# New durations, hand-over times and a new transfer rate in the table of an attention-and-feed-forward kernel's scheduler

## The chip, the core and the metric

The kernel runs on one core of one Trainium2 chip. It uses TensorE (PE in the profile; its weight loads are PEld), VectorE (DVE), ScalarE (ACT), GpSimd (POOL) and SyncE (SP), which here issues nearly all transfers. The metric is the device time of one execution in microseconds, as the median of several runs.

## What is computed

Two layers, one behind the other. The first is linear attention with random features, on 8 batch entries of 8 heads, 576 positions and 64 dimensions:

```python
def phi(x):
    proj = np.einsum('bhsd,md->bhsm', x, omega)
    sq = np.sum(x * x, axis=-1, keepdims=True) / 2.0
    h = proj - sq
    h = h - np.max(h, axis=-1, keepdims=True)
    return np.exp(h) / np.sqrt(m)
q_p, k_p = (phi(q_s), phi(k_s))
kv = np.einsum('bhsm,bhsd->bhmd', k_p, v)
z = np.sum(k_p, axis=2)
num = np.einsum('bhsm,bhmd->bhsd', q_p, kv)
den = np.einsum('bhsm,bhm->bhs', q_p, z)[..., None] + 1e-06
return (num / den).astype(np.float32)
```

The second takes the attention's output as 4608 tokens of 512 values and puts them through a feed-forward layer with 2048 inner values:

```python
h = x @ w_in
sp = np.maximum(h, 0.0) + np.log1p(np.exp(-np.abs(h)))
g = h * erf(sp)
return (g @ w_out).astype(np.float32)
```

## The kernel before

**Tiling.** The heads are taken in pairs, four pairs to each of the 8 batch entries, 32 pairs in all. For a pair, `load` brings keys and queries (uk, uq) and values (v) and squares them into the other half of the same tile (`sqk`, `sqq`). `project` multiplies in three groups of 384 rows (PSUM tiles ppk, ppq), takes the row maxima (mxk, mxq on DVE) and the exponentials (fk, fq on ACT). `key_values` sums keys times values (kvp, copied to kh, kl). `turn` transposes the query features (pt, copied to qh, with the remainder ql). `attend` multiplies both (nd), takes the reciprocal (rc, on ACT as logarithm and exponential) and divides (xs, on DVE).

The feed-forward layer runs for each batch entry in two phases of four blocks. Operands are split in a high part and a remainder (xh and xl, gh and gl, and both in each weight tile w), and each product is three matmuls: high by high, high by low, low by high. The first three batch entries multiply in the plain way (`plain1`, tiles h). From the fourth on, `gemm1` uses a Strassen scheme with seven products (tiles hS and hA, helper u). `chain` then computes softplus and erf (gs, on ACT, with table loads), the gate (hs), and the split. `gemm2` multiplies by the output weights (tiles o, copied or added to os, stored by `ostore`). The weights are unpacked once in `make` (a load to st, a bias to wt, three steps in pw, then `parts` into w), stored to DRAM, and fetched again from there for every later use (`fetch`).

**What sets the order.** No order is written out by hand. `build` lists every operation with the engines that may run it, a duration for each (the second number of each option) and a slack from which that option may be used. `Plan.order` then plays the program through: it keeps a time for each engine, gives each idle engine the ready operation that is due first, and writes down the sequence. An operation becomes ready after its producers, plus LAG of the producing engine. PSUM banks and buffers are handed out in the same play: a new tile waits until all users of a freed one are done. For SP it assumes that a transfer ends 2 us after a bandwidth clock (`bw`) that advances by size over a rate. The program is then emitted in that sequence, each engine in order, with `keep_in_program_order`. So durations in the table don't set any time on the chip; they set which engine runs an operation, which operation stands ahead of which on an engine, and which PSUM bank and buffer a tile gets.

**Lines of the profile.** All instructions are recorded by one helper, so nearly every row has line L755; rows are told apart by the names of their tiles. Buffer numbers are left out in the profile.

Of the kernel before, what the change touches and what calls it, by code (L numbers as in the profile page):

```python
# [59 lines left out]
LAG = {"T": 0.35, "A": 0.25, "V": 0.25, "G": 0.3, "S": 0.3}  # L60
# [29 lines left out]
class Plan:  # L90
# [43 lines left out]
    def order(self, slots, caps):  # L134
# [192 lines left out]
def build(emit):  # L327
# [36 lines left out]
    def parts(t, src, keys, psum=False):  # L364

        ks = range(2)
        pl.op("whigh", [("A", 0.58, -1e9), ("V", 0.62, WHV)] if psum else
              [("A", 0.63, -1e9), ("G", 0.7, WHG)], lambda e: E.w_high(e, t, src),
              reads=keys, writes=[(t, ("h", k)) for k in ks])
        pl.op("wlow" if psum else "wrest",  # L370
              [("V", 0.68, -1e9)] if psum else [("V", 0.68, -1e9), ("G", 1.3, 3.0)], lambda e: E.w_rest(e, t, src),
              reads=keys + [(t, ("h", k)) for k in ks], writes=[(t, ("l", k)) for k in ks])

    def make(u, t):
# [6 lines left out]
        pl.op("wbias", [("G", 0.8, WBG), ("A", 0.67, -1e9)], lambda e: E.w_bias(e, st, w),  # L381
# [5 lines left out]
        pl.op("wsign", [("V", 0.72, -1e9)], lambda e: E.w_sign(st, p), reads=[(st, 0), (p, 0)],  # L387
# [19 lines left out]
    def make_sums(ph, fp, t0, t1):  # L407

        r = pl.tile("gh", f"R{ph}_{fp}", [P, 2, 2, BW], F32, "wt")
        for i, t in enumerate((t0, t1)):  # L410
            pl.op("wwhole", [("V", 0.68, -1e9), ("G", 1.3, 3.0)],
                  lambda e, i=i, t=t: E.w_whole(e, r.ap[:, i], t),
                  reads=[(t, (x, k)) for x in "hl" for k in range(2)], writes=[(r, i)])
        s = pl.tile("gl", f"S{ph}_{fp}", [P, 4, BW], F32, "st")

        for x, y, sign, keys, to in (
# [4 lines left out]
            pl.op("wsum", [("V", 0.37, -1e9), ("G", 0.75, 3.0)],  # L421
# [51 lines left out]
    def project(n, qk, t0):  # L473
# [5 lines left out]
        for i in range(3):  # L479
# [4 lines left out]
            pl.op("max" + qk, [("V", 0.56, -1e9)], lambda e, i=i, pp=pp: E.maximum(mx, pp, i),  # L484
                  reads=[(pp, 0)], writes=[(mx, i)])
            pl.op("exp" + qk, [("A", 1.1, -1e9)], lambda e, i=i, pp=pp: E.exponential(f, mx, pp, i),
                  reads=[(pp, 0), (mx, i)], writes=[(f, i)], set="exp")

    def key_values(n, t0):
# [10 lines left out]
        pl.op("kvhigh", [("V", 0.6, -1e9), ("A", 0.7, -1e9)], lambda e: E.kv_high(e, kh, kvp),  # L500
              reads=[(kvp, 0)], writes=[(kh, 0)])
        if not whole:
            pl.op("kvrest", [("V", 0.6, -1e9)], lambda e: E.kv_rest(kl, kvp, kh),
                  reads=[(kvp, 0), (kh, 0)], writes=[(kl, 0)])

    def turn(n, t0):
# [5 lines left out]
        for i in range(3):  # L512
# [3 lines left out]
            pl.op("turnhigh", [("A", 0.5, -1e9), ("V", 0.5, -1e9)],  # L516
                  lambda e, i=i, pt=pt: E.turn_high(e, qh, pt, i), reads=[(pt, 0)], writes=[(qh, i)])
            if not whole:
                pl.op("turnrest", [("V", 0.56, -1e9)], lambda e, i=i, pt=pt: E.turn_rest(ql, qh, pt, i),
                      reads=[(pt, 0), (qh, i)], writes=[(ql, i)])  # L520

    def attend(n, t0):
        a = pairs[n]
        x = xs[n] = pl.tile("xs", f"xs{a['nm']}", [P, 2, T])
        for t in range(2):
# [83 lines left out]
    def plain1(b, ph, fp):  # L609
# [3 lines left out]
        for i in range(2):  # L613
            for t in range(2):
# [3 lines left out]
                pl.op("hout", [("A", 0.42, -1e9), ("V", 0.46, 0.0)],  # L618
# [3 lines left out]
    def gemm1(b, ph, fp):  # L622
# [25 lines left out]
    def chain(b, ph, fps):  # L648
# [25 lines left out]
    def gemm2(b, ph, et):  # L674
# [378 lines left out]
```

## Time and profile before

| | |
|---|---|
| time, median of 3 runs | 1087.89 us (1086.58 to 1088.42) |
| span of the profiled execution, first to last instruction | 1083.2 us |
| its own time beside the span | not listed; the median is 4.7 us over the span |
| transfers | 231.27 MB, 213 GB/s on average |
| fetches of 512 KB weight tiles, issue to landing | 4.4 us in the median (184 of them) |
| table loads on ACT | 91, 1283 ns each |

The profile is of one execution. A row of the timeline gives start, length, engine, line, operation, output and inputs, the count of instructions merged, and in brackets the idle time of the engine ahead of it with what ended it. Matmul ends are modelled, so the start of the next matmul tells more than the end of the last. In the windows a row gives the stretch, its length, the busy time of PE, PEld, DVE, ACT and POOL with instruction counts, the granted TensorE clock, the DMA engines' share and the GB/s moved.

### The profile page before, as it was taken

Reading aid. Unit: us, or ns where it says so; the run is one execution under the profiler, and the core shown is the slowest. Engines: PE = TensorE matmul, PEld = TensorE weight load, DVE = VectorE, ACT = ScalarE, POOL = GpSimd, SP = SyncE. Lnnn points to the kernel's source line nnn. Section 1 sums busy time; section 2 is a strip of 40 time slices with the busy share of each in tenths; the row PEclk is TensorE's granted clock in tenths of the full one; section 3 lists DMA queues with packets and bytes.
Section 4 is the critical chain, followed back from the end, with each engine's and each line's share of the span. In section 5 each row is a group of like instructions: output and inputs, shape, how many; then the busy total and the mean of one; then the engine's idle time right before and its main releaser. Section 6 shows DMA issues by size and latency. Waiting matters only on the chain.

```text
span 1083.2 us, 21493 instructions
## 1 busy us (share of the span) xinstructions
PE 1066.8 (98%) x8272; PEld 1059.2 (98%) x8272; DVE 724.0 (67%) x1302; ACT 672.6 (62%) x1262; POOL 462.6 (43%) x362
## 2 busy tenths in 40 slices
PE   7899999999999999999999999999999999999998
PEld 7799999999999999999999999999999999999998
DVE  5999988683585676946667565766657757565541
ACT  7768876576676685647647555675556665564440
POOL 5436336352294673815335334452435412253300
PEclk9999999999999999999999999999999999999999
DMA  8465676676367676568765766667765766667771
GB/s 235 162 210 177 221 265 223 227 274 200 115 218 240 225 234 202 177 206 255 226 208 183 248 226 223 187 211 233 230 210 182 241 203 197 216 229 265 264 240 52
DMA packets 70117, 231.27 MB, mean 213 GB/s; under 512 B 8288, under 2 KB 8672, under 8 KB 70016
## 3 DMA queue, kind: packets, MB, share of 16 engines
q1 hardware_dynamic: 69952, 229.84, 64.9%
q8 instruction: 66, 1.08, 0.4%
q14 instruction: 35, 0.29, 0.1%
q0 software_dynamic: 64, 0.07, 0.0%
HBM read 195.26 MB, written 34.60 MB: 212 GB/s over the span
## 4 chain that ended last, share of the span: by engine, by line
PE 94%; DVE 4%; ACT 1%; issue 0%; DMA 0%; DVEq 0%; POOLq 0%
PE o L755 37%; PE h L755 14%; PE hS L755 12%; PE hA L755 9%; PE ppk L755 6%; PE ppq L755 6%; PE kvp L755 5%; PE nd L755 5%; PE pt L755 2%; DVE mxk L755 0%; DVE xl L755 0%; DVE pw L755 0%; DVE gl L755 0%; DVE xc L755 0%; DVE qh L755 0%
## 5 line engine op out<-in xcount | busy, mean ns | idle before, releaser
L755 PE MATMUL o<-gh,w 128*128 128x288 f32 x2048 | 442.3, 298 | 1.9 <-DVE ql L755 1.0
L755 PEld LDWEIGHTS o<-gh,w 128*128 128x128 f32 x2048 | 338.3, 188 | 2.5 <-PE o L755 1.2
L755 PE MATMUL o<-gl,w 128*128 128x288 f32 x1024 | 301.8, 295 | 0.0
L755 PEld LDWEIGHTS o<-gl,w 128*128 128x128 f32 x1024 | 192.7, 188 | 0.1
L755 PE MATMUL h<-xh,w 128*128 128x288 f32 x768 | 176.0, 303 | 0.6 <-DVE hs L755 0.6
L755 PE MATMUL hS<-xh,wS 128*128 128x288 f32 x640 | 160.0, 299 | 1.1 <-DVE u L755 1.1
L755 POOL TENSOR_TENSOR hs<-gs,hs 128x576 f32<-128x576 f32 x64 | 101.4, 1607 | 105.7 <-ACT gs L755 68.9
L755 POOL TENSOR_TENSOR gl<-hs,gh 128x576 fp32r<-128x576 f32 x66 | 117.9, 1810 | 33.0 <-ACT gh L755 25.7
L755 PEld LDWEIGHTS h<-xh,w 128*128 128x128 f32 x768 | 129.1, 188 | 1.5 <-DVE hs L755 0.8
L755 ACT ACTIVATE fk<-ppk,mxk 128x128 f32<-128x128 f32 x288 | 82.2, 375 | 74.8 <-DVE mxk L755 74.5
L755 PE MATMUL hA<-xh,w 128*128 128x288 f32 x480 | 122.8, 300 | 0.0
L755 ACT ACT_TABLE_LOAD x91 | 116.8, 1283 | 4.3 <-DVE hs L755 2.0
L755 PEld LDWEIGHTS hS<-xh,wS 128*128 128x128 f32 x640 | 112.9, 188 | 1.3 <-DVE u L755 1.3
L755 POOL TENSOR_TENSOR uq<-uq 64x576 f32<-64x576 f32 x42 | 49.7, 1201 | 150.3 <-DMA uq<-qT 105.3
L755 PE MATMUL h<-xl,w 128*128 128x288 f32 x384 | 113.0, 294 | 0.0
L755 ACT ACTIVATE fq<-ppq,mxq 128x128 f32<-128x128 f32 x288 | 81.6, 372 | 30.4 <-DVE mxq L755 30.2
L755 DVE TENSOR_REDUCE mxk<-ppk 128x3 f32<-128x384 f32 x96 | 52.4, 555 | 62.6 <-PE ppk L755 61.3
L755 PE MATMUL hS<-xl,wS 128*128 128x288 f32 x320 | 94.2, 294 | 0.0
L755 POOL TENSOR_TENSOR uk<-uk 64x576 f32<-64x576 f32 x46 | 52.4, 1159 | 86.1 <-DMA uk<-kT 60.8
L755 PEld LDWEIGHTS hA<-xh,w 128*128 128x128 f32 x480 | 85.5, 188 | 0.1
L755 DVE TENSOR_TENSOR os<-o,os 128x288 f32<-128x288 f32 x64 | 29.0, 455 | 83.5 <-PE o L755 83.5
L755 PE MATMUL ppk<-wk,uk 128*128 128x128 f32 x576 | 78.1, 280 | 4.1 <-DVE wk L755 4.0
(94 smaller groups left out, 2084.6 us busy)
## 6 DMA issues: line engine op xcount, KB each, us to landing
w<-wdw SPq DMA_DIRECT2D x184, 512.0 KB, 4.4
wS<-wdcS SPq DMA_DIRECT2D x80, 512.0 KB, 4.0
st<-w SPq DMA_DIRECT2D x32, 512.0 KB, 4.5
wdw<-w SPq DMA_DIRECT2D x32, 512.0 KB, 4.2
v<-vP SPq DMA_DIRECT2D x32, 325.0 KB, 3.6
w<-wdw SPq DMA_DIRECT2D x40, 256.0 KB, 3.5
out<-os SPq DMA_DIRECT2D x32, 288.0 KB, 3.5
uk<-kT SPq DMA_DIRECT2D x31, 288.0 KB, 3.8
```

Source lines behind the costliest of these rows:

```text
L755: return tc.keep_in_program_order(method(*args, **kwargs))
```

## The change

The table gets new numbers, and nothing else is touched. LAG of ACT, DVE and POOL goes up, the rate of transfers goes from 230 to 300 KB per us, most durations of DVE and ACT go down by 0.05 to 0.3 us, and some of POOL go up. The core of the diff:

```diff
-LAG = {"T": 0.35, "A": 0.25, "V": 0.25, "G": 0.3, "S": 0.3}
+LAG = {"T": 0.35, "A": 0.35, "V": 0.33, "G": 0.33, "S": 0.3}
...
-                        bw = begin + o.size / 230e3
+                        bw = begin + o.size / 300e3
...
-            pl.op("max" + qk, [("V", 0.56, -1e9)], lambda e, i=i, pp=pp: E.maximum(mx, pp, i),
+            pl.op("max" + qk, [("V", 0.47, -1e9)], lambda e, i=i, pp=pp: E.maximum(mx, pp, i),
```

In the same way: exponentials 1.1 to 0.77, `turnhigh` on ACT 0.5 to 0.39, `kvhigh` 0.6 and 0.7 to 0.4, evacuations of PSUM on DVE 0.46 to 0.38 and on ACT 0.42 to 0.34, `sp` and `erf` 1.2 to 1.1, `wbias` on POOL 0.8 to 0.65, `rest` on POOL 2.75 to 2.95, `recip` 1.45 to 1.5.

This moves operations between engines (`turnhigh` on ACT from 37 to 58 of 96, `wbias` on ACT from 5 to 17 of 32) and shifts rows on all of them. Three places follow. In their names the first number of a pair's tile is the pair within its batch entry (qh_0 is pair 0; weights wt, st and w have other numbers), the last a running number.

ACT, in the first batch entry, from the square of a later key tile to the exponentials of pair 1's queries. Before:

```order
L755 ACTIVATE uk_0_118<-uk_0_118 64x1152
L755 ACTIVATE fk_1_214<-ppk_1_0_187,mxk_1_200 128x128 x3
L755 ACTIVATE qh_0_229<-pt_0_1_218 128x384
L755 ACTIVATE fk_1_214<-ppk_1_1_196,mxk_1_200 128x128 x3
L755 ACTIVATE fk_1_214<-ppk_1_2_203,mxk_1_200 128x128 x3
L755 ACTIVATE uq_0_141<-uq_0_141 64x1152
L755 ACTIVATE rc_0_0_266<-nd_0_0_0_233,eps 64x288
L755 ACTIVATE rc_0_0_266<-nd_0_1_0_238,eps 64x288
L755 ACTIVATE rc_0_0_266<-rc_0_0_266 128x288
L755 ACTIVATE fq_1_276<-ppq_1_0_249,mxq_1_258 128x128 x3
```

With the change, from the row behind the same square on:

```order
L755 ACTIVATE uk_2_126<-uk_2_126 64x1152
L755 ACTIVATE fk_1_222<-ppk_1_0_187,mxk_1_201 128x128 x3
L755 ACTIVATE qh_0_230<-pt_0_2_226 128x384
L755 ACTIVATE fk_1_222<-ppk_1_1_197,mxk_1_201 128x128 x3
L755 ACTIVATE fk_1_222<-ppk_1_2_203,mxk_1_201 128x128 x3
L755 ACTIVATE wt_0_0_250<-st_0_0_150 128x512
L755 ACTIVATE rc_0_0_256<-nd_0_0_0_234,eps 64x288
L755 ACTIVATE rc_0_0_256<-nd_0_1_0_239,eps 64x288
L755 ACTIVATE rc_0_0_256<-rc_0_0_256 128x288
L755 ACTIVATE rc_0_1_275<-nd_0_0_1_246,eps 64x288
L755 ACTIVATE rc_0_1_275<-nd_0_1_1_248,eps 64x288
L755 ACTIVATE rc_0_1_275<-rc_0_1_275 128x288
```

The three exponentials fq_1 come directly behind these, then the square of uq_3 and the bias wt of the third weight tile, then fk_2. A second square and a weight bias came to ACT (from POOL), and both reciprocals now stand ahead of fq_1.

DVE, from the third weight tile's first step to the copies of pair 2's turned queries. Before:

```order
L755 TENSOR_SCALAR pw_0_2_454<-wt_0_2_375 128x512
L755 TENSOR_REDUCE mxk_3_460<-ppk_3_0_437 128x3
L755 TENSOR_REDUCE mxk_3_460<-ppk_3_1_448 128x3
L755 COPY qh_2_479<-pt_2_0_462 128x384
L755 COPY qh_2_479<-pt_2_1_467 128x384
L755 TENSOR_REDUCE mxk_3_460<-ppk_3_2_456 128x3
L755 SCALAR_TENSOR_TENSOR pw_0_2_454<-st_0_2_297,pw_0_2_454 128x512 x2
```

With the change:

```order
L755 TENSOR_SCALAR pw_0_2_440<-wt_0_2_343 128x512
L755 SCALAR_TENSOR_TENSOR pw_0_2_440<-st_0_2_297,pw_0_2_440 128x512 x2
L755 TENSOR_REDUCE mxk_3_461<-ppk_3_0_442 128x3
L755 TENSOR_REDUCE mxk_3_461<-ppk_3_1_452 128x3
L755 TENSOR_REDUCE mxk_3_461<-ppk_3_2_457 128x3
L755 COPY qh_2_485<-pt_2_0_463 128x384
L755 COPY qh_2_485<-pt_2_2_480 128x384
```

All three weight steps and all three maxima now stand ahead of the copies. A little later on ACT, the square of a query tile of the second batch entry (uq_1) comes to stand directly ahead of the two reciprocals of pair 3, where before no square stood.

PE, at the step from the plain to the Strassen batches, from the last turn of a pair to its products nd. Before, 13 rows of the output tile o lie between; these are the last five with the product behind them:

```order
L755 MATMUL o_0_3_1_5503<-gl_0_2_4716,w_0_3_1_88_5193 128x288
L755 MATMUL o_0_3_1_5503<-gh_0_2_4638,w_0_3_1_88_5193 128x288
L755 MATMUL o_0_3_1_5503<-gh_0_3_4746,w_0_3_1_88_5193 128x288
L755 MATMUL o_0_3_1_5503<-gl_0_3_4791,w_0_3_1_88_5193 128x288
L755 MATMUL o_0_3_1_5503<-gh_0_3_4746,w_0_3_1_88_5193 128x288
L755 MATMUL nd_0_0_0_5546<-qh_0_5457,kh_0_5364 128x288
```

With the change:

```order
L755 MATMUL hA_0_0_5549<-xh_1_5331,w_0_0_89_5264 128x288
L755 MATMUL pt_0_2_5563<-ident,fq_0_5271 128x128 x3
L755 MATMUL nd_0_0_0_5575<-qh_0_5558,kh_0_5361 128x288
L755 MATMUL nd_0_0_0_5575<-ql_0_5571,kh_0_5361 128x288
L755 MATMUL nd_0_0_0_5575<-qh_0_5558,kl_0_5367 128x288
L755 MATMUL nd_0_1_0_5582<-qh_0_5558,kh_0_5361 128x288
L755 MATMUL nd_0_1_0_5582<-ql_0_5571,kh_0_5361 128x288
```

The last turn now stands directly ahead of the products, and the output tile's matmuls stand ahead of all three turns.

More of the change, by code (lines that the diff above doesn't have):

```diff
@@ L483, in project @@
                   plan=pair_time(n, t0 + 0.05 * i))
-            pl.op("max" + qk, [("V", 0.56, -1e9)], lambda e, i=i, pp=pp: E.maximum(mx, pp, i),
+            pl.op("max" + qk, [("V", 0.47, -1e9)], lambda e, i=i, pp=pp: E.maximum(mx, pp, i),
                   reads=[(pp, 0)], writes=[(mx, i)])
-            pl.op("exp" + qk, [("A", 1.1, -1e9)], lambda e, i=i, pp=pp: E.exponential(f, mx, pp, i),
+            pl.op("exp" + qk, [("A", 0.77, -1e9)], lambda e, i=i, pp=pp: E.exponential(f, mx, pp, i),
                   reads=[(pp, 0), (mx, i)], writes=[(f, i)], set="exp")
@@ L499, in key_values @@
         kl = a["kl"] = kh if whole else pl.tile("kl", "kl" + a["nm"], [P, 2, P], F32R)
-        pl.op("kvhigh", [("V", 0.6, -1e9), ("A", 0.7, -1e9)], lambda e: E.kv_high(e, kh, kvp),
+        pl.op("kvhigh", [("V", 0.4, -1e9), ("A", 0.4, -1e9)], lambda e: E.kv_high(e, kh, kvp),
               reads=[(kvp, 0)], writes=[(kh, 0)])
         if not whole:
-            pl.op("kvrest", [("V", 0.6, -1e9)], lambda e: E.kv_rest(kl, kvp, kh),
+            pl.op("kvrest", [("V", 0.4, -1e9)], lambda e: E.kv_rest(kl, kvp, kh),
                   reads=[(kvp, 0), (kh, 0)], writes=[(kl, 0)])
@@ L540, in attend @@
             for j in range(2):
-                pl.op("divide", [("V", 0.47, -1e9)],
+                pl.op("divide", [("V", 0.4, -1e9)],
                       lambda e, j=j, t=t, nd=nds[j], rc=rc: E.divide(x, nd, rc, j, t),
@@ L663, in chain @@
             four = [(g["hs"], (i, t)) for i in range(2) for t in range(2)]
-            pl.op("gate", [("V", 1.36, -1e9), ("G", 2.75, GATES if (b, ph) >= EARLY else GATES0)], lambda e, g=g: E.gate(e, g["gs"], g["hs"]),
+            pl.op("gate", [("V", 1.27, -1e9), ("G", 2.78, GATES if (b, ph) >= EARLY else GATES0)], lambda e, g=g: E.gate(e, g["gs"], g["hs"]),
                   reads=four + [(g["gs"], 0)], writes=four)
             g["gh"] = pl.tile("gh", f"gh{b}_{ph}_{fp}", [P, 2, 2, T], F32R, cap=4 if b < PLAIN or (b, ph) == (PLAIN, 0) else None)
-            pl.op("high", [("V", 0.76, -1e9), ("A", 1.17, 3.0)], lambda e, g=g: E.high(e, g["gh"], g["hs"]),
+            pl.op("high", [("V", 0.68, -1e9), ("A", 1.08, 3.0)], lambda e, g=g: E.high(e, g["gh"], g["hs"]),
                   reads=four, writes=[(g["gh"], 0)])
             g["gl"] = pl.tile("gl", f"gl{b}_{ph}_{fp}", [P, 2, 2, T], F32R, cap=4 if b < PLAIN or (b, ph) == (PLAIN, 0) else None)
-            pl.op("rest", [("G", 2.75, RESTS if (b, ph) >= EARLY else RESTS0), ("V", 1.36, -1e9)],
+            pl.op("rest", [("G", 2.95, RESTS if (b, ph) >= EARLY else RESTS0), ("V", 1.3, -1e9)],
                   lambda e, g=g: E.rest(e, g["gl"], g["hs"], g["gh"]),
```

34 lines of the change are left out of this document (17 added, 17 removed).

## The prediction

> **What bounds the kernel now.** I read the head of the page first, then the busy time by stage, then the TensorE timeline at the few places where it waits.
>
> ```profile
> span 1083.2 us, 21493 instructions
> PE 1066.8 (98%) x8272; PEld 1059.2 (98%) x8272; DVE 724.0 (67%) x1302; ACT 672.6 (62%) x1262; POOL 462.6 (43%) x362
> PE 94%; DVE 4%; ACT 1%; issue 0%; DMA 0%; DVEq 0%; POOLq 0%
> 0.00:54.00 54.00, 45.52 (x321) 41.38 (x322) 40.94 (x86) 42.06 (x120) 28.73 (x37) 1.00 0.68 198
> 54.00:108.00 54.00, 54.00 (x418) 53.12 (x418) 49.27 (x85) 42.78 (x82) 26.88 (x23) 1.00 0.59 195
> 540.00:1026.00 486.00, 486.00 (x3796) 485.93 (x3794) 310.61 (x595) 283.81 (x489) 189.05 (x134) 1.00 0.68 220
> ```
>
> PE (TensorE) is busy 98% of the span, and all of 540 to 1026 us (the first numbers of a window's row are its length and PE's busy time). The change alters neither the matmuls nor their count, so what it can win is PE's idle time: 1083.2 - 1066.8 = 16.4 us, of which 54.0 - 45.5 = 8.5 lie in the first 54 us. Four of these are the start, before the first projection, and the end has its own 3.6 (the last store), which no order changes. What is left are single waits. These are the rows that carry them; a bracket is idle time and what ended it.
>
> ```profile
> 4.01 4.18 PE L755 MATMUL ppk<-wk,uk 128*128 128x128 f32 x18 [4.01 <-DVE wk L755]
> 12.78 2.23 PE L755 MATMUL ppk<-wk,uk 128*128 128x128 f32 x18
> 16.12 2.30 PE L755 MATMUL nd<-qh,kh 128*128 128x288 f32 x8
> 21.27 2.22 PE L755 MATMUL kvp<-v,fk 128*128 128x130 f32 x18 [0.84 <-ACT fq L755]
> 32.97 2.22 PE L755 MATMUL kvp<-v,fk 128*128 128x130 f32 x18 [0.41 <-DVE xs L755]
> 38.24 2.31 PE L755 MATMUL nd<-qh,kh 128*128 128x288 f32 x8
> 48.85 0.72 PE L755 MATMUL nd<-qh,kh 128*128 128x288 f32 x2 [1.05 <-DVE qh L755]
> 53.50 1.60 PE L755 MATMUL ppq<-wq,uq 128*128 128x128 f32 x12 [0.36 <-DVE xs L755]
> 56.90 2.23 PE L755 MATMUL ppk<-wk,uk 128*128 128x128 f32 x18
> 125.99 0.40 PE L755 MATMUL h<-xh,w 128*128 128x288 f32 x1 [0.55 <-DVE hs L755]
> 165.89 0.40 PE L755 MATMUL o<-gh,w 128*128 128x288 f32 x1 [0.88 <-ACT os L755]
> 444.08 0.37 PE L755 MATMUL o<-gh,w 128*128 128x288 f32 x1 [1.02 <-DVE ql L755]
> 452.93 0.40 PE L755 MATMUL hS<-xh,wS 128*128 128x288 f32 x1 [1.09 <-DVE u L755]
> 517.97 0.40 PE L755 MATMUL nd<-qh,kh 128*128 128x288 f32 x1 [0.18 <-ACT qh L755]
> 518.74 0.40 PE L755 MATMUL nd<-ql,kh 128*128 128x288 f32 x1 [0.37 <-DVE ql L755]
> ```
>
> A bracket leaves out the tail of the matmul before it, about 0.16 us; start against start the waits behind 54 us cost 0.7, 1.0, 1.2, 1.25 and 1.0 (the last two rows together): 5.2 us. That is all a better order could win there.
>
> **The change part by part.** Only numbers in the scheduler's table change; all instructions keep their form, some change engine, and the order of each engine's rows follows.
>
> *Do the new numbers fit the trace?* A maximum is 0.56 in the old table and 0.47 in the new one.
>
> ```profile
> L755 DVE TENSOR_REDUCE mxk<-ppk 128x3 f32<-128x384 f32 x96 | 52.4, 555 | 62.6 <-PE ppk L755 61.3
> 36.48 1.01 DVE L755 TENSOR_REDUCE mxk<-ppk 128x3 f32<-128x384 f32 x2
> 39.03 1.41 DVE L755 SCALAR_TENSOR_TENSOR pw<-st,pw 128x512 int32<-128x512 int32 x2
> 37.62 1.02 DVE L755 COPY qh<-pt 128x384 f32<-128x384 f32 x2
> ```
>
> One lasts 555 ns, but two take 1.01 us: the second starts 0.46 after the first. The new entries are such start-to-start times, and the 0.08 us taken off stands in LAG (0.25 to 0.33 for V). [...]
>
> *The first 60 us, by the orders of ACT and DVE in the section on the change.* Now ACT, POOL and the queue there:
>
> ```profile
> 13.59 1.16 ACT L755 ACTIVATE uk<-uk 64x1152 f32<-64x1152 f32 x1 [0.98 <-DMA uk<-kT]
> 15.70 0.49 ACT L755 ACTIVATE qh<-pt 128x384 f32<-128x384 f32 x1
> 16.09 1.65 ACT L755 ACTIVATE fk<-ppk,mxk 128x128 f32<-128x128 f32 x6
> 18.95 1.02 ACT L755 ACTIVATE rc<-nd,eps 64x288 f32<-64x288 f32 x2
> 20.35 2.42 ACT L755 ACTIVATE fq<-ppq,mxq 128x128 f32<-128x128 f32 x9
> L755 ACT ACTIVATE wt<-st x5: 657/665/682, 93.4 to 221.6; 128x512 f32<-128x512 f32 x5
> 14.84 2.25 POOL L755 TENSOR_TENSOR uk<-uk 64x576 f32<-64x576 f32 x2 [0.80 <-DMA uk<-kT]
> 20.50 0.47 SPq L755 DMA_DIRECT2D uq<-qT  x1
> DMA to landing us min/median/max: 6.5/6.5/6.5
> 46.04 0.47 SPq L755 DMA_DIRECT2D uq<-qT  x1
> 50.07 2.25 POOL L755 TENSOR_TENSOR uq<-uq 64x576 f32<-64x576 f32 x2 [0.83 <-DMA uq<-qT]
> ```
>
> 1. ACT gets a second square, uk_2, ahead of pair 1's exponentials. Its load lands at 14.8 (the POOL row). So square to 15.95, exponential 0.89, copy of the turned queries to 17.4 (before 16.2); pair 0's second product nd, at 16.7 before, starts at 17.4: +0.7.
> 2. Then two exponentials to 18.95, the weight bias wt 0.66 to 19.6, both reciprocals (1.49 each) to 22.6, and only now fq_1, the first to 23.5. Its bank is what kvp of pair 1 waits for: 23.6 against 21.27, +2.3.
> 3. fq_1 ends at 25.1. Next in ACT's queue is the square of uq_3, whose load was issued at 20.50 and landed 6.5 later, at 27.0, with the DMA engines full; square and second bias end at 28.9, and fk_2 starts there, not at 25.9. PE has kvp (2.1), ppk (2.0) and the turn (1.0) to do, then waits for the DVE copies, to 30.0; four nd (2.3 together) and ppq (2.0) follow, kvp of pair 2 starts at 33.5: +0.5 only, since before it waited for the divides until 32.97.
> 4. DVE takes the weight chain pw (0.68 + 1.41) and three maxima (1.5) ahead of pair 2's copies: from 35.9 to 39.4, first copy done 39.85, nd at 39.9 against 38.24: +1.7.
> 5. Pair 3 keeps this (kvp 44.05, before 42.4), but the wait at 48.85 shrinks: the next batch's ppq starts at 52.1, before 51.7: +0.4.
> 6. ACT now squares uq_1 ahead of pair 3's reciprocals. The load is issued when ppk has read the buffer, 48.3 by this count, and takes 3.9 to 4.0 (46.04 to 50.07): 52.2; square 53.4, reciprocal 54.9, divide 55.4. The second ppq needs that bank: 55.4 against 53.50; ppk of the next pair comes at 59.2 against 56.90. Sum of the stage: **+2.3 us**. Bounds: -1 if the queues are a microsecond earlier than I count (before's recoverable waits there are 5 us), +4 if loads take 2 us more.
>
> *The places behind 54 us.* At 125.99 and 517.97 the new order has over 0.5 us more cover between producer and consumer; at 165.89 the two evacuations "os" leave ACT for DVE. These three go: **-2.7**. At the step to the Strassen batches (444 and 453) the turns stand directly ahead of the products nd. From the last turn, copy 0.49, remainder 0.55 and some 0.2 of hand-over (1.24) face one nd of three matmuls and one more, 4 x 0.13 = 0.5: a wait of 0.8 takes the place of 1.2 + 1.25: **-1.6**; bounds -2.4 and +1, as DVE may be late with its backlog. One fetch loses cover:
>
> ```profile
> 961.10 1.11 SPq L755 DMA_DIRECT2D w<-wdw  x2
> DMA to landing us min/median/max: 3.3/3.3/3.3
> 965.67 0.29 PE L755 MATMUL o<-gh,w 128*128 128x288 f32 x1
> ```
>
> Landed at 964.4, used at 965.67; the new order has four groups of three matmuls less between (1.58 us): **+0.3**. In three earlier batches it loses one group (0.4 of at least 1.5): nothing.
>
> *What I can't read from the order.* Two of the five old waits (1.0, 1.25) came from a queue, not from too little cover, and the new order will have its own. I allow one, **+1.1** (bounds 0 and +4).
>
> Sum against the span: 2.3 - 2.7 - 1.6 + 0.3 + 1.1 = -0.6, so 1082.6; with the 4.7 between span and median (1087.89 - 1083.2), **1087.3 us**.
>
> **The rivals.**
>
> *Closer numbers close the waits* (0.27): the first 60 us come out level and no new queue wait appears: -2.7 - 1.6 - 1 to -5, about 1082.5. For it: LAG is now nearer to what a hand-over costs, and most entries fit. Against it: the loads on which ACT now waits.
>
> *ACT waits in order behind transfers* (0.25, the slower side): besides step 6, squares stand directly ahead of a reciprocal at five places behind 470 us where none stood before. Counted like the step at 450, a reciprocal there has 0.4 us of cover if the load lands 4.5 us after its issue; the mechanism decides from 4.9. The loads I see took 3.9 and 6.5. At 6.5 each costs 1.6, together 8, and with the rest 1095; at 3.9 nothing, as I forecast.
>
> *The table is not what the trace shows* (0.04): if DVE operations did cost 0.56, each run of three maxima or six turn operations would come 0.25 to 0.5 us late, for 24 pairs up to 12 us: 1099. [...]
>
> *A wait cools TensorE* (0.04): the first 18 ppk took 4.18 us, later ones 2.23, with the granted clock at 1.00 throughout. If the wait of step 2 grew by a microsecond and the rate fell again, one such stretch more costs 2 us: 1089.3. [...]
>
> **How the numbers follow.** My forecast has 0.40, with a range of its own from 1085 to 1090. Faster by over 0.2% (below 1085.7; about what a measurement can tell from no change) is the first rival and a little of the forecast: 0.30; within 0.2% 0.39; slower (above 1090.1) 0.31. Leaving out the outer tenth on each side: 1082 to 1095.
>
> **What would show it.** In the new profile: ACT idle before a square until its DMA at about 27 and 52 us; kvp of pair 1 at 23.6 and ppk of the second batch's pair 1 at 59.2; PE idle gone at 126, 166 and 518; one wait of about 0.8 before "nd" near 450; a short one near 965. I am wrong if the first 60 us take no longer than before, or if PE shows new waits in the stretch from 540 to 960, where I expect none.

## The result and the profile after

The changed kernel takes 1093.34 us in the median of 7 runs (1090.68 to 1094.68), the kernel before 1087.92 (1086.58 to 1089.04): a ratio of 1.0051, 95% interval 1.0039 to 1.0062. It is 5.4 us slower; the forecast was 0.6 us faster. A few executions in the runs below took 1.4 to 2.5 times as long, whatever the kernel; medians and ratios leave them out.

Each run of the changed kernel is listed with its span and the mean granted TensorE clock. The time is 1.8 us above the span in all of them, and it follows the clock:

| time, us | 1090.68 | 1090.78 | 1092.19 | 1093.34 | 1094.34 | 1094.65 | 1094.68 |
|---|---|---|---|---|---|---|---|
| span, us | 1088.9 | 1089.0 | 1090.4 | 1091.5 | 1092.6 | 1092.8 | 1092.9 |
| clock | 0.998 | 0.998 | 0.996 | 0.995 | 0.995 | 0.995 | 0.994 |

The profile is of the last one, the slowest of the seven. Its span is 9.7 us over that of the profile before (1083.2), more than the 5.4 us between the medians. The head of its page:

```profile
span 1092.9 us, 21440 instructions
PE 1072.2 (98%) x8272; PEld 1063.4 (97%) x8272; DVE 713.5 (65%) x1264; ACT 705.8 (65%) x1328; POOL 421.2 (39%) x327
PE 93%; DVE 3%; ACT 1%; DMA 1%; issue 1%; SPq 1%; DVEq 0%
```

PE's busy time grew by 5.4 us (1072.2 against 1066.8) with the same matmuls: some ran slower. Windows of the changed kernel (busy time by engine, then the granted clock) say where:

```profile
0.00:54.00 54.00, 43.16 (x307) 39.23 (x308) 39.22 (x79) 42.51 (x122) 19.82 (x26) 0.97 0.69 193
54.00:108.00 54.00, 52.03 (x377) 50.97 (x375) 45.79 (x79) 42.64 (x83) 21.34 (x19) 0.94 0.59 201
108.00:162.00 54.00, 51.50 (x380) 49.72 (x379) 48.07 (x76) 40.75 (x97) 23.18 (x21) 0.97 0.67 222
540.00:1026.00 486.00, 485.75 (x3786) 484.86 (x3786) 311.00 (x579) 297.04 (x513) 168.09 (x125) 1.00 0.67 219
```

Behind 540 us nothing is lost, as before. In each of the first three windows PE idles more and its clock is below 1.00; before, the first two showed 1.00. In steps of 3 us the clock falls at three places:

```profile
18.00:21.00 3.00, 3.00 (x6) 2.16 (x7) 0.00 (x0) 1.96 (x7) 3.00 (x4) 0.50 1.04 235
57.00:60.00 3.00, 2.85 (x19) 2.85 (x20) 2.88 (x7) 2.68 (x9) 0.28 (x1) 0.75 0.29 116
60.00:63.00 3.00, 3.00 (x16) 3.00 (x16) 1.95 (x4) 1.30 (x6) 2.62 (x4) 0.50 0.55 163
63.00:66.00 3.00, 3.00 (x18) 3.00 (x18) 0.78 (x2) 0.75 (x4) 2.18 (x2) 0.61 0.38 111
114.00:117.00 3.00, 3.00 (x18) 3.00 (x17) 2.47 (x5) 2.12 (x6) 2.77 (x3) 0.57 0.35 78
```

And these are PE's rows of the timeline that answer to the waits of before (brackets are idle time):

```profile
17.98 3.19 PE L755 MATMUL nd<-qh,kh 128*128 128x288 f32 x6 [2.19 <-ACT qh L755]
25.04 2.22 PE L755 MATMUL kvp<-v,fk 128*128 128x130 f32 x18 [1.86 <-ACT fq L755]
35.43 2.12 PE L755 MATMUL kvp<-v,fk 128*128 128x130 f32 x18
42.12 2.18 PE L755 MATMUL nd<-qh,kh 128*128 128x288 f32 x8 [1.53 <-DVE qh L755]
57.15 1.71 PE L755 MATMUL ppq<-wq,uq 128*128 128x128 f32 x12 [1.97 <-DVE xs L755]
58.65 3.95 PE L755 MATMUL kvp<-v,fk 128*128 128x130 f32 x18
112.25 0.40 PE L755 MATMUL h<-xh,w 128*128 128x288 f32 x1 [2.48 <-DVE w L755]
459.74 0.40 PE L755 MATMUL nd<-qh,kh 128*128 128x288 f32 x1 [0.99 <-ACT fk L755]
460.71 0.40 PE L755 MATMUL nd<-ql,kh 128*128 128x288 f32 x1 [0.18 <-DVE ql L755]
973.61 0.37 PE L755 MATMUL o<-gh,w 128*128 128x288 f32 x1 [0.19 <-DMA w<-wdw]
```

The reader is to see two things. Three waits of 2 to 2.5 us stand at 15.8, 55.2 and 109.8, each followed, at once or within two microseconds, by a stretch at half rate: six nd take 3.19 us where eight took 2.30, and 18 kvp take 3.95 where they took 2.22. And the wait of 1.86 ahead of kvp at 25.04 has no half rate behind it.

### The profile page after: what moved, and what is told of

Its sections match the earlier page's. It is cut to its first block, busy times and chain, and to the rows that moved or that the text cites. A ratio compares the mean times of both kernels' runs of the same rounds, so it can differ in the third digit from the quotient of the medians.

```text
span 1092.9 us, 21440 instructions
## 1 busy us (share of the span) xinstructions
PE 1072.2 (98%) x8272; PEld 1063.4 (97%) x8272; DVE 713.5 (65%) x1264; ACT 705.8 (65%) x1328; POOL 421.2 (39%) x327
## 4 chain that ended last, share of the span: by engine, by line
PE 93%; DVE 3%; ACT 1%; DMA 1%; issue 1%; SPq 1%; DVEq 0%
PE o L755 37%; PE h L755 13%; PE hS L755 11%; PE hA L755 9%; PE ppq L755 5%; PE kvp L755 5%; PE ppk L755 5%; PE nd L755 4%; PE pt L755 2%; DVE pw L755 1%; DMA uk<-kT 1%; SPq L755 1%; ACT rc L755 0%; DVE w L755 0%; DVE xs L755 0%
## 5 line engine op out<-in xcount | busy, mean ns | idle before, releaser
L755 PE MATMUL hS<-xh,wS 128*128 128x288 f32 x640 | 164.5, 301 | 0.0
L755 ACT ACTIVATE gh<-hs 128x1152 fp32r<-128x1152 f32 x52 | 59.4, 1164 | 34.1 <-POOL hs L755 21.5
L755 POOL TENSOR_TENSOR uq<-uq 64x576 f32<-64x576 f32 x36 | 40.5, 1144 | 105.8 <-DMA uq<-qT 84.4
```

The lines of the kernel that those rows point to most:

```text
L755: return tc.keep_in_program_order(method(*args, **kwargs))
```

## The experiments

The moves below use a small helper: `put(a, b)` takes row a out of the sequence that the scheduler's play wrote down and sets it behind row b (with `ahead=True`, ahead of it). Nothing else changes, tiles and buffers included. Times are medians, ratios are against the kernel before in the same session.

### Half rate

**e1_before**: no edit.

> The kernel before, unchanged, for its spans and granted clocks run by run. In the seven runs of the changed kernel the time is 1.8 us above the span, and the clock is 0.994 to 0.998. If the same 1.8 holds here, the profiled execution of before (span 1083.2, clock 0.999) stood for 1085.0, and the runs at 1087.9 have spans near 1086: then their clock should be lower than 0.999 (0.996 to 0.998: 2 to 3 us of half rate that the profiled execution didn't have). Rival: the clock is 0.999 in all of them, and the difference between profile and median is something else.

Ratio 0.9995 (0.9986 to 1.0004). The time is 1.8 to 2.1 us above the span here too; spans go from 1083.4 to 1086.5, clocks from 0.998 to 1.000. So the profiled execution of before was one of its shortest, and of the 4.7 us between it and the median some 2 are outside the span and some 2.7 belong to that one execution. Low clocks explain part of these only: runs at 1.000 had spans up to 1085.7.

**e2_filler**:

```diff
+    FILL = (("projq", "ppq_0_1_2", 6), ("projq", "ppq_1_0_0", 5), ("projq", "ppq_1_2_0", 7))
+    def filler(t, n):
+        for _ in range(n):
+            pe.matmul(t.ap[:, 384:512], lhsT=wk, rhs=wq, start=True, stop=True)
...
+        if o is find("nd", "nd_0_0_1_0"):
+            filler(o.uses[-1], 7)
```

> The changed kernel with 25 more matmuls of 128x128 (0.22 us each, 5.5 us in all), whose results nothing reads, put where TensorE waits: 7 in the wait at 15.4, 6 at 22.9, 5 at 54.9, 7 at 109.5 us. No wait of the other engines changes. Theory 'a wait cools TensorE': no stretch at half the granted clock is left after these waits, clock 0.999 in every run, and the time falls by the 2.2 to 6.6 us that the clocks of 0.998 to 0.994 stand for: about 1087 (ratio 1.000), with the runs within 1.5 us of each other. Rival 'the half rate has another cause' (load, time): the half-rate stretches stay, the time is 1093 or, where a filler holds something up, above.

1090.76 us (ratio 1.0039, 1.0024 to 1.0053). Five of six runs have a clock of 0.999 or 1.000 and lie within 1.1 us; the sixth has 0.996 and takes 1095.6. The windows of this run at the old places:

```profile
18.00:21.00 3.00, 3.00 (x23) 2.77 (x22) 0.63 (x2) 2.21 (x7) 2.88 (x3) 1.00 1.05 268
60.00:63.00 3.00, 3.00 (x28) 3.00 (x28) 2.91 (x6) 1.98 (x9) 2.68 (x3) 1.00 0.64 186
113.00:116.00 3.00, 3.00 (x29) 3.00 (x29) 2.93 (x6) 2.43 (x8) 0.00 (x0) 1.00 0.97 325
```

23, 28 and 29 rows of PE pass where 6, 16 and (in 114 to 117) 18 did. The rows are not all of the same products, so the clock is the surer sign: it is 1.00. More work in the waits, and the half rate behind them is gone: it comes from the waits. What that is worth is less sharp. By the medians it is 2.6 us (1093.34 to 1090.76), by the ratios 1.3 with overlapping intervals, since they count the sixth run. It is less than the 6 expected. Above before 2.9 us are left by the medians (4.2 by the ratio), with waits but at full clock.

**e11_probe** (one execution): the kernel before with a product on PE that waits for n fills on POOL, at twelve places.

```diff
+        if id(o) in stops:
+            pe.matmul(o.alloc[0].ap[:, 384:512], lhsT=wk, rhs=scratch[:, :P], start=True, stop=True)
+            for _ in range(stops[id(o)]):
+                pool.memset(scratch, 0.0)
+            pe.matmul(o.alloc[0].ap[:, 384:512], lhsT=wk, rhs=scratch[:, :P], start=True, stop=True)
```

> The kernel before with twelve waits put into TensorE's steady stretch from about 555 us on, 36 us apart: a small product waits for 4 to 24 fills of a 128x128 tile on GpSimd (about 0.2 us each), so waits of about 1 to 6 us, in mixed order. Theory 'a wait cools TensorE, from a certain length on': matmul intervals of twice 132 ns for some us behind every wait longer than about 2.1 us, none behind those under 1.8. Rival 'the length decides only together with when the wait falls': between about 1.5 and 3.5 us some waits are followed by half rate and some not. [...]

Four of the waits (their length is in the bracket), and the windows directly behind them, in the same order:

```profile
789.84 0.49 PE L755 MATMUL hS<-om,wk 128*128 128x128 f32 x2 [1.69 <-POOL om L755]
881.77 0.49 PE L755 MATMUL hA<-om,wk 128*128 128x128 f32 x2 [2.42 <-POOL om L755]
968.96 0.63 PE L755 MATMUL hA<-om,wk 128*128 128x128 f32 x2 [2.94 <-POOL om L755]
1060.55 0.49 PE L755 MATMUL hS<-om,wk 128*128 128x128 f32 x2 [1.89 <-POOL om L755]
```

```profile
789.90:793.00 3.10, 3.10 (x26) 3.10 (x26) 0.46 (x1) 1.57 (x2) 2.25 (x2) 1.00 0.45 154
881.90:885.00 3.10, 3.10 (x25) 3.10 (x26) 1.92 (x2) 0.00 (x0) 2.57 (x2) 1.00 0.03 5
969.10:972.30 3.20, 3.20 (x15) 3.20 (x16) 1.20 (x3) 0.00 (x0) 0.00 (x0) 0.51 0.05 15
1060.70:1064.10 3.40, 3.40 (x18) 3.40 (x19) 0.91 (x2) 0.00 (x0) 0.00 (x0) 0.59 0.28 92
```

Half rate follows the wait of 1.89 and not the one of 2.42. Behind 1.11 and 1.69 there was none (clock 1.00); behind 2.94, 3.20, 3.67 and 3.72 there was (0.51, 0.68, 0.50 and 0.55). So much of the second theory holds: in between, length alone does not decide. What else decides is not shown. In the other runs 2.57 (e4_square), 2.63 (e13_four_places) and even 3.29 (e5_norate) passed without; behind the first and the last of these the clock was 1.00. Shorter ones than 1.89 were followed by half rate there: 1.77 in e4_square (clock 0.51 from 18 to 21), 1.53 in e6_rate (0.59 from 39 to 42) and 1.37 in e5_norate, where 18 kvp take 2.85 us for 2.22 and the clock from 24 to 27 is 0.55:

```profile
21.89 2.85 PE L755 MATMUL kvp<-v,fk 128*128 128x130 f32 x18 [1.37 <-ACT fq L755]
```

So waits from about 1.4 to 3.3 us can go either way here.

### The three places

**e3_wlow**: `put(("wlow", "pw2_0_0_0"), ("high", "gh0_0_2"), ahead=True)`

> The changed kernel with one DVE row moved: the low part of the weight tile that frees a PSUM bank stands ahead of the cast gh, not behind it. The wait of 2.65 us at 109.5 becomes about 1.2. Theory 'wait and cooling': 1.45 less wait and 1.7 less half rate, -3.1: 1090.2. Rival 'only the wait counts': -1.45, 1091.9. Rival 'something else is late next': no gain, 1093.3.

1092.55 us (1.0048, 1.0037 to 1.0060). The one wait of 2.48 became three:

```profile
110.31 0.40 PE L755 MATMUL h<-xh,w 128*128 128x288 f32 x1 [0.86 <-DVE w L755]
112.39 1.58 PE L755 MATMUL ppq<-wq,uq 128*128 128x128 f32 x12 [0.62 <-ACT fq L755]
115.43 2.27 PE L755 MATMUL kvp<-v,fk 128*128 128x130 f32 x18 [1.07 <-DVE hs L755]
```

Their sum, 2.55, is what there was, and half rate follows these three short waits too:

```profile
117.00:120.00 3.00, 3.00 (x18) 3.00 (x18) 2.66 (x5) 1.75 (x7) 0.31 (x1) 0.58 1.03 345
```

In e10_places (below) nearly the same three waits (0.91, 0.62 and 1.07) have the clock at 1.00 behind them. By the trace "something else is late next" is right; the time alone can't tell it from "only the wait counts".

**e4_square**:

```diff
+    put(("sqq", "uq_1_1"), ("recip", "rc_0_3_1"))
+    put(("whigh", "pw1_0_4"), ("divide", "nd_0_3_1_0"))
+    put(("maxq", "ppq_1_0_0"), ("divide", "nd_0_3_1_0"))
```

> The changed kernel with the square of uq_1 (second batch) behind the two reciprocals of pair 3 on ACT, and on DVE one weight step and one maximum behind the divides. The wait of 2.24 us at 54.9 becomes about 1.0. Theory 'wait and cooling': the products behind it start about 0.6 us earlier and the 3.4 us of half rate between 58 and 66 us go: -4, 1089.3. Rival 'only the wait counts': -0.6, 1092.7. Rival 'DVE is late next': nothing, 1093.3.

1091.11 us (1.0035, 1.0021 to 1.0049): by the medians 2.2 faster than the changed kernel, between the theories (the intervals overlap). The wait of 1.97 became 0.41 and 0.80 (the latter for a weight step on DVE), and the window from 60 to 63 has clock 1.00.

**e9_place1** (two squares and the first weight bias later in ACT's order) and **e10_places** (this with the moves of e3 and e4):

```diff
+    put(("sqk", "uk_1_0"), ("expk", "ppk_0_1_2"))
+    put(("sqk", "uk_0_2"), ("expk", "ppk_0_1_2"))
+    put(("wbias", "wt1_0_0"), ("expq", "ppq_0_1_2"))
+    for step in ("wtail", "wsign", "wshift"):
+        put((step, "pw1_0_0"), ("divide", "nd_0_0_1_1"))
```

> The changed kernel with its order repaired at one place, the first 25 us: on ACT the squares of uk_0 (second batch) and uk_2 stand behind pair 1's exponentials, the first weight bias behind pair 1's query exponentials, and on DVE its three steps behind pair 0's divides. Theory 'loads that land later than the table has it hold ACT': the wait of 2.5 at 15.4 and the half rate behind it go, the products kvp of pair 1 start at 21 to 22 (25.0 in the changed kernel, 21.3 before), and pairs 2 and 3 keep 1 to 2 us of that; with the other waits left, 1090. Rival 'something else is late next': kvp of pair 1 moves, pair 3 doesn't, 1093.

> The changed kernel with all three places repaired (the one of e9_place1, the square and two DVE rows of e4_square, the DVE row of e3_wlow). If the parts add up (-3, -2.2 and -0.8 against 1093.3): 1087.3, level with before, clock 0.998 or more. Rival 'something else is late next': 1090 or more, with waits of over 1.5 us at other places in the first 120 us.

1093.71 us (1.0068, 1.0055 to 1.0080) and 1091.92 (1.0052, 1.0038 to 1.0066). In e9 the nd no longer wait, but the next product does, and half rate follows it (18 kvp in 4.11 us); ACT's row shows why:

```profile
24.07 4.11 PE L755 MATMUL kvp<-v,fk 128*128 128x130 f32 x18 [3.78 <-ACT fq L755]
18.00 2.21 ACT L755 ACTIVATE uk<-uk 64x1152 f32<-64x1152 f32 x2
```

The two squares now stand between pair 1's exponentials and pair 0's reciprocals, and cost 2.2 us of ACT there. The expectation of 21 to 22 overlooked this. e10 keeps this wait of 3.78 us and the half rate behind it, so its rival, "something else is late next", fits.

**e12_act_order** and **e13_four_places**: ACT's first 30 us in about the order of before, and then all places at once. Of the 11 and 18 moves these are some; the last two lines are of e13 alone.

```diff
+    put(("sqk", "uk_1_0"), ("expk", "ppk_0_2_2"))
+    put(("sqq", "uq_0_3"), ("expk", "ppk_0_2_2"))
+    put(("recip", "rc_0_0_1"), ("expq", "ppq_0_1_2"))
+    put(("wbias", "wt1_0_0"), ("expq", "ppq_0_1_1"))
...
+    for step in ("wtail", "wsign"):
+        put((step, "pw1_0_2"), ("turnhigh", "pt_0_2_2"))
```

> The changed kernel with the first 30 us in another order, after e9_place1 left a wait of 3.9 us there: on ACT only the square of uk_2 stands ahead of pair 1's exponentials, pair 0's second reciprocal stands behind pair 1's query exponentials, the first weight bias between their second and third; the squares of uk_0 (second batch) and uq_3 and the next bias stand behind pair 2's exponentials. Theory 'ACT's own rows ahead of fq_1 (a second square 1.1, a second reciprocal 1.5) make kvp of pair 1 late, not a late load': it starts at 21 to 22 with a wait of about 1, no half rate before 50 us, pair 2 at 33 to 34; with the waits at 55 and 109 left, 1089 to 1091. Rival 'the loads': kvp of pair 1 stays at 24, 1093.

> The order of e12_act_order, two weight steps behind the turned copies of pair 2 on DVE (the wait of 1.7 at 40), and the moves of e4_square and e3_wlow. If the waits are what made the changed kernel slower: 1086 to 1088, level with before or a little under it, clock 0.998 or more. Rival 'something else is late next': 1090 or more.

1091.82 us (1.0050, 1.0035 to 1.0064) and 1092.60 (1.0049, 1.0036 to 1.0062). In e12, kvp of pair 1 starts at 21.45, as the theory on ACT's own rows had it. But pair 3 is later than in the changed kernel (table below), and the time is not the 1089 to 1091 of that theory. Waits came back at other places, most of them on DVE. e13's five runs have clocks of 0.998 and 0.999 and still take some 5 us more than before: there the loss is waits at full clock (9.7 us from 5 to 60 us in its profile, 4.2 before). No repair by hand, of 1 to 18 rows, reached the time of before.

### The parts of the table

**e5_norate**, **e6_rate**, **e7_dur**, **e8_lag** (and **e14_lag_again** for its profile):

```diff
 e5_norate: after
-                        bw = begin + o.size / 300e3
+                        bw = begin + o.size / 230e3
 e6_rate: before
-                        bw = begin + o.size / 230e3
+                        bw = begin + o.size / 300e3
 e7_dur: after
-LAG = {"T": 0.35, "A": 0.35, "V": 0.33, "G": 0.33, "S": 0.3}
+LAG = {"T": 0.35, "A": 0.25, "V": 0.25, "G": 0.3, "S": 0.3}
-                        bw = begin + o.size / 300e3
+                        bw = begin + o.size / 230e3
 e8_lag, e14_lag_again: before
-LAG = {"T": 0.35, "A": 0.25, "V": 0.25, "G": 0.3, "S": 0.3}
+LAG = {"T": 0.35, "A": 0.35, "V": 0.33, "G": 0.33, "S": 0.3}
```

> The changed kernel with the transfer rate of the table back at 230 KB per us; LAG and durations stay new. In its order one square and no weight bias stand ahead of pair 0's reciprocals on ACT, as before the change; the square of uq_1 stays ahead of pair 3's. Theory 'the rate does not fit the first 25 us, where the traces show 180 to 280 KB per us': the waits at 15.4 and 22.9 (2.5 and 2.0) shrink to those of before (0.3 and 1.0), and no half rate between 18 and 21; time about 1089. Rival 'durations or LAG make the first waits': the two waits stay, 1093. Rival 'any new order has waits of its own': the first waits go, others of 2 us come elsewhere, 1091 to 1094.

> The kernel before with the new rate alone. In its order a weight bias stands ahead of pair 0's first reciprocal, but only one square ahead of pair 1's exponentials. Theory 'the rate does not fit the first 25 us': ACT waits for the third load of weights (landing near 20.5), the products kvp of pair 1 start 2 to 3 us later than before's 21.3, with half rate behind some of the waits: 1090 to 1092. Rival 'the rate does nothing by itself': 1087.5. Rival 'it helps': below 1086.

> The kernel before with the new durations alone. Theory 'the rate is to blame': the first 25 us are as before (waits at 16 and 20 of 0.3 and 1.0), and what is left is the waits behind 100 us; 1086 to 1088. Rival 'any new order has waits of its own': waits of 2 us at new places and half rate behind them, 1090 to 1093. By the first rival of the prediction (closer numbers close the waits) it would be 1083.

> The kernel before with the new LAG alone. Theory 'the rate is to blame': first 25 us as before; longer hand-overs in the table give more cover, 1085 to 1088. Rival 'any new order has waits of its own': 1090 to 1093.

> The kernel of e8_lag again (new LAG alone), for a profile that is not disturbed. By its time in e8_lag (1095.2, clock 0.994 to 0.999): two or three waits of over 2 us in the first 120 us with half rate behind them, at other places than in the changed kernel.

| table | time, us | ratio to before | 95% interval |
|---|---|---|---|
| new durations alone (e7) | 1088.41 | 1.0008 | 0.9998 to 1.0019 |
| new rate alone (e6) | 1092.47 | 1.0050 | 1.0035 to 1.0065 |
| new LAG alone (e8) | 1094.91 | 1.0063 | 1.0044 to 1.0083 |
| durations and LAG (e5) | 1096.60 | 1.0080 | 1.0065 to 1.0095 |
| all three (the change) | 1093.34 | 1.0051 | 1.0039 to 1.0062 |

The durations cost nothing that these runs can tell; rate and LAG each cost 5 us or more, and they don't add up. e14_lag_again, one execution of the new LAG alone, took 1093.85 us with a clock of 0.998; it has one wait of over 2 us (2.86, ahead of kvp of pair 1) and not the two or three that were expected, so with some 2 us of half rate (0.002 of the span) most of its loss is waits. e6 shows the first wait of the changed kernel at the same place and size, made by the rate alone:

```profile
15.45 1.16 ACT L755 ACTIVATE uk<-uk 64x1152 f32<-64x1152 f32 x1 [3.74 <-DMA uk<-kT]
17.94 3.20 PE L755 MATMUL nd<-qh,kh 128*128 128x288 f32 x6 [2.17 <-ACT qh L755]
```

ACT stands idle for 3.74 us ahead of a square whose load isn't there. The reason is in the play: with 230 it has the early loads land within 2 us of the trace of before, with 300 it has them 4 to 8 us earlier than the trace of after. Landings in us, of the play with either rate, and measured:

| load | play, 230 (before) | measured, before | play, 300 (after) | measured, after |
|---|---|---|---|---|
| uk of pair 2 | 13.0 | 14.8 | 11.2 | 15.5 |
| first weights st | 17.9 | 18.7 | 14.9 | 20.5 |
| v of pair 2 | 22.9 | 24.5 | 18.7 | 26.1 |
| uk of pair 3 | 24.2 | 26.0 | 19.7 | 27.6 |
| uq of pair 3 | 25.4 | 27.0 | 21.2 | 28.6 |

Each measured column is one profile, and landings spread. The first 15 loads that SP issues are the same in every run here, the first weights being the last of them, issued at 9.4 to 9.7 us; yet these weights landed between 18.6 (e9_place1) and 22.4 (e14_lag_again). For them the play is 0.8 to 4.5 us early in the kernels made with 230, and 3.7 to 7.2 in those made with 300.

e5_norate, though, has the first 20 us of before and is the slowest of all: a wait of 1.77 ahead of kvp of pair 2, of 1.84 near 56 and of 3.29 at 106. "Any new order has waits of its own" was the theory that fitted it.

### Work on POOL

At equal progress of PE (321 rows) the two profiles compare like this, before (54 us, quoted in the prediction) and after:

```profile
0.00:58.00 58.00, 45.20 (x321) 40.97 (x322) 42.81 (x85) 46.34 (x128) 19.82 (x26) 0.97 0.67 188
```

POOL did 28.73 us of work before and 19.82 now; ACT went from 42.06 to 46.34, DVE from 40.94 to 42.81. **e15_pool** (whole new table), **e16_dur_pool** (new durations alone), **e17_norate_pool** (new durations and LAG) and **e18_before_pool** (old table) take ACT out of the options of two operations there:

```diff
-        pl.op("wbias", [("G", 0.65, WBG), ("A", 0.6, -1e9)], lambda e: E.w_bias(e, st, w),
+        pl.op("wbias", [("G", 0.65, WBG), ("A", 0.6, -1e9)][:1 if u[:2] == ("1", 0) else 2], lambda e: E.w_bias(e, st, w),
...
-                  [("G", 2.2, SQG if n < SQN else -1e9), ("A", 1.2, -1e9 if n < SQN else SQA)],
+                  [("G", 2.2, SQG if n < SQN else -1e9), ("A", 1.2, -1e9 if n < SQN else SQA)][:1 if n < 2 * NP else 2],
```

> The changed kernel (whole new table) with ACT struck from the options of two operations of the first two batch entries: their squares (from the second pair on) and the biases of the first eight weight tiles run on POOL alone. At equal progress of TensorE (its first 321 rows, 54 us before and 58 after) POOL's busy time fell from 28.7 to 19.8 us with the change and ACT's rose from 42.1 to 46.3. Theory 'work that left POOL for ACT is what fills the first 60 us': POOL back near 28 us, ACT near 42, kvp of pairs 1 to 3 at 21 to 22, 33, 43 and the next batch at 55 to 56; with the waits near 109 and 458 left, 1088 to 1090. Rival 'every new order has waits of its own there': kvp of the next batch 4 us late again, 1091 or more.

> The same two options struck, with the new durations alone (LAG and rate as before the change; e7_dur with POOL). Theory 'work that left POOL': a little faster than e7_dur's 1088.4, 1086 to 1088. Rival 'every new order has waits of its own there': 1090 or more.

> e15_pool with the rate back at 230 KB per us (new LAG and durations, the two options struck from ACT). By the traces, the play with 230 puts the landings of the first 30 us within 2 us of the measured ones, with 300 it puts them 5 to 8 us early (uk of pair 3: 19.7 in the play, 27.6 measured). Theory 'the late landings make the wait of 6.8 us at 28.6 in e15': that wait goes, no wait over 2 us in the first 60 us, 1087 to 1089. Rival 'the new LAG brings the waits': 1091 or more, as in e5 and e8.

> The kernel before, old table, with only the two options struck from ACT. Theory 'the option is what helps, whatever the table': 1085 to 1087, level with e16_dur_pool's 1086.2. Rival 'it needs the new durations': 1088 or more. Tells whether anything of the new table is worth keeping.

| table, with POOL | time, us | ratio to before | 95% interval |
|---|---|---|---|
| whole new table (e15) | 1092.37 | 1.0052 | 1.0035 to 1.0069 |
| durations and LAG (e17) | 1091.16 | 1.0036 | 1.0022 to 1.0051 |
| durations (e16) | 1086.01 | 0.9989 | 0.9980 to 0.9998 |
| old table (e18) | 1086.52 | 0.9996 | 0.9986 to 1.0005 |

In e15 the early waits are gone and one of 6.65 us takes their place. Its chain, from the last link back: kvp on PE, a weight step on DVE with the maxima queued behind it, and POOL, which stood in order before a square whose load landed at 27.3:

```profile
35.53 2.83 PE L755 MATMUL kvp<-v,fk 128*128 128x130 f32 x12 [6.65 <-ACT fq L755]
32.67 0.69 DVE L755 TENSOR_SCALAR pw<-wt 128x512 int32<-128x512 int32 x1 [7.64 <-POOL wt L755]
27.33 2.25 POOL L755 TENSOR_TENSOR uk<-uk 64x576 f32<-64x576 f32 x2 [3.27 <-DMA uk<-kT]
```

With the rate at 230 (e17) this wait is gone, as the theory of late landings had it; waits of 2.06 at 37 and of 1.81 at 101 are left, and the time lies where the rival (the new LAG brings the waits) had it. With the old LAG too (e16) no wait of the first 60 us behind the start is over 1.4. e16 beats the changed kernel by 0.6% and the kernel before by 0.1%. e18 can't be told from e16 or from before.

How late the first group of kvp of each pair starts against before (21.3, 33.0, 42.4 and, for the next batch entry, 54.9 us), from the timelines:

| | pair 1 | pair 2 | pair 3 | next batch |
|---|---|---|---|---|
| after | +3.8 | +2.5 | +3.8 | +3.7 |
| e7_dur | +1.6 | +1.4 | +2.5 | +1.1 |
| e6_rate | +2.2 | +3.2 | +5.0 | +4.8 |
| e14_lag_again | +3.2 | +4.2 | +4.3 | +4.2 |
| e5_norate | +0.6 | +1.9 | +3.7 | +5.0 |
| e12_act_order | +0.2 | +1.7 | +4.9 | +5.1 |
| e13_four_places | +1.1 | +2.5 | +6.1 | +5.5 |
| e15_pool | -1.9 | +2.6 | +5.6 | +5.1 |
| e17_norate_pool | -1.3 | -3.3 | -0.1 | +0.2 |
| e16_dur_pool | -0.7 | -2.7 | -1.9 | -2.3 |
| e18_before_pool | -0.6 | -2.0 | +0.5 | -0.8 |

Every order of this table whose interval lies above 1 is 3.7 us or more late at the next batch, except e17, whose loss lies mostly behind 90 us.

## Why the prediction was wrong

| term | predicted, us | measured, profile against profile |
|---|---|---|
| second ppq of the next batch | +1.9 (55.4) | +3.65 (57.15 against 53.50) |
| half rate from 57 to 66 | 0 | +3.4 (3 us times 0.25, 0.50 and 0.39) |
| waits at 125.99, 165.89, 517.97 | -2.7 | -2.7: no row has a bracket there |
| one new queue wait | +1.1 | +2.65 start to start, at 109.5 |
| half rate behind it | 0 | +1.7 (3 us times 0.14 and 0.43) |
| 444 and 453 | -1.6 | -0.95 (1.15 + 0.34 for 2.44) |
| fetch near 965 | +0.3 | +0.35 at 973 |

The measured column adds up to 8.1 of the 9.7 us between the two spans; 1.6 lie in small pieces that were not followed.

**Right:** the waits behind 120 us. Three went, one wait of two parts stands at the transition, the fetch costs a third of a microsecond, and 540 to 960 shows none. ACT waits before squares for their loads in the first 60 us, as steps 1 and 6 said.

**Wrong, put at nothing:** half rate. The rival "a wait cools TensorE" stood at 0.04 and at one stretch of 2 us, and only if the wait of step 2 grew by a microsecond. That it had to grow was the author's assumption, and no run shows it. The sum itself forecast a wait of about 2 us (step 2: kvp at 23.6 against 21.27), and waits of this size can be long enough: 1.97, 2.19 and 2.48 were each followed by half rate, though the one of step 2 (1.86) was not. e2_filler shows that the half rate comes from the waits, and 1.3 to 2.6 us of the 5.4; by the clocks of the seven runs (0.994 to 0.998, so 0.006 to 0.002 of the span) it is 6.6 to 2.2. The two counts are not reconciled. Part of the difference is that a later wait shrinks: from 18 to 21 half rate takes 1.5 us, but with fillers the next kvp starts only 0.84 earlier (24.20 in e2_filler, 25.04 in the changed kernel). No single length parts the waits with half rate behind them from those without: 1.89 us was enough in e11_probe and 1.37 in e5_norate, while 2.42 and 3.29 in the same two runs were not. Why is not shown.

**Wrong, sized too small, and by the medians the larger part:** the waits of the first 60 us. e2_filler, at full clock, is 2.9 us over before where 0.6 under it was forecast, so some 3.5 of the 6.0 us that the forecast missed are waits, these and the new queue wait below. In its profile the second ppq of the next batch starts at 56.24, +2.74 against the +1.9 of step 6. One cause is step 2. It had the weight bias run when ACT reached it; instead ACT stood 1.04 us idle for the weights, which landed at 20.5. Step 1 had the load at 14.8, the landing of before; it was 15.5. The slip is the same: a landing time of one old profile was taken as fixed. The order does not explain these two, since the queue holds the same loads ahead of them in both kernels; from profile to profile the first weights land up to 3.8 us apart (18.6 to 22.4, above). With the half rate at 18 to 21 this makes kvp at 25.04 for 23.6.

```profile
14.33 2.31 ACT L755 ACTIVATE uk<-uk 64x1152 f32<-64x1152 f32 x2 [2.33 <-DMA uk<-kT]
20.52 0.66 ACT L755 ACTIVATE wt<-st 128x512 f32<-128x512 f32 x1 [1.04 <-DMA st<-w]
53.94 1.16 ACT L755 ACTIVATE uq<-uq 64x1152 f32<-64x1152 f32 x1 [0.67 <-DMA uq<-qT]
```

**Wrong, not asked:** "Do the new numbers fit the trace?" was answered for DVE's durations alone. There the answer held: the new durations cost less than 0.2% (e7), not the 12 us of the rival. No run shows that each maximum costs DVE the 0.56 which that rival counts with: in the trace of before the second of two starts 0.46 us after the first (36.48, two in 1.01). The rate was left out of that question. 300 KB per us does not fit the first 30 us, where the loads queue (the DMA engines' share is 0.96 to 1.04 from 6 to 24 us of the changed kernel, at 217 to 277 GB/s): the play is 4 to 8 us early there (within 2 with 230 in the profile of before). The rival "the table is not what the trace shows" was right for the rate, by another row than the one it named.

**Right in kind, too small:** the new queue wait. Start to start it cost 2.65 us for 1.1. It is a weight step on DVE behind a gate of 2.24 us and a cast (rows in the last section).

**The 4.7 us** between span and median mixed 1.8 to 2.1 us that every run has with 2.7 that belonged to that one execution (e1_before). The difference to before is not touched by it.

**Open:** why the new LAG brings waits of about 2 us and more in three tables (e8, by its repeat e14; e5; e17). The prediction held it to be nearer to what a hand-over costs. The trace of before does not show that: from the start of a row maximum on DVE to the exponential on ACT that waits for it there are 0.58 us (25.35 to 25.93; 0.57 to 0.60 in the 61 that waited so), and duration and LAG add up to 0.81 in the old table and to 0.80 in the new one. That the new LAG brings these waits is shown; which rows do it was not taken apart.

## What to carry to other kernels

A scheduler's table is not judged by whether each number is measured, but by whether the play then hits the landings and waits of the trace where the machine is tight; here, with the new rate, the play was 4 to 8 us early in the first 30 us, where the DMA engines' share was 0.96 to 1.04 from 6 to 24. When an order is changed, list the waits that the new order will have, and price those on TensorE with a possible stretch at half rate behind them: here it followed waits from 1.37 us on (e5_norate), and once three close together of 0.86, 0.62 and 1.07 (e3_wlow). And before rows are moved by hand, look at the work of each engine: moving rows on ACT and DVE, busy for 42.5 and 39.2 of the changed kernel's first 54 us, moved the wait (3.78 us ahead of kvp in e9). Moving work to POOL, busy for 19.8, cut PE's waits from 5 to 60 us from 6.6 to 3.4 us with the new durations alone (e7 and e16), but with the whole new table it made one of 6.65 us (e15).

## What was not expected of the hardware

The length of a wait does not decide alone whether half rate follows (1.89 us in e11_probe did it, 2.42 did not), and the same kernel ran with clocks of 0.994 to 0.998 and times 4 us apart. Half-rate stretches of the changed kernel lasted some 3 us (18 to 21, 113 to 116) or twice that (58.7 to 65).

A gate on DVE took 2.24 us beside POOL, where half of another gate ran until 108.8 and then a weight bias, which took 1.76. The median is 1.39 for the 32 such gates on DVE and 0.66 for the 15 such biases on POOL. Three gates on DVE with nothing on POOL beside them took 1.35 (at 481.53, 546.37 and 936.04). The one here ended at 110.02, 1.2 us behind POOL's gate, and POOL's bias at 110.53, 0.5 behind DVE's; what held the two is not shown. The scheduler's play lengthens operations that run beside each other on the two engines (in `Plan.order`, those listed in `SHARED`); the prediction did not count with that. DVE's rows of the changed kernel behind 107 us, and POOL's:

```profile
107.78 2.24 DVE L755 TENSOR_TENSOR hs<-gs,hs 128x1152 f32<-128x1152 f32 x1
109.94 1.20 DVE L755 CAST gh<-hs 128x1152 fp32r<-128x1152 f32 x1
111.06 0.54 DVE L755 TENSOR_REDUCE mxq<-ppq 128x3 f32<-128x384 f32 x1
111.52 0.67 DVE L755 TENSOR_TENSOR w<-pw,w 128x512 fp32r<-128x512 f32 x1
108.77 1.76 POOL L755 TENSOR_SCALAR wt<-st 128x512 f32<-128x512 f32 x1
```

The last DVE row is the one that PE waited for until 112.25.
